# First batch of a spectral mixture-of-experts kernel: fixed load order, stage hand-over through DRAM, deeper input buffers

## The chip, the cores and the metric

The kernel runs on one core of a Trainium2 chip. The metric is the device time of one execution in microseconds (us), the median of several runs. The engines are called as in the profile: PE (matrix products) with its weight loads PEld, DVE (vector), ACT (scalar), POOL (GpSimd) and SP, which computes nothing here and issues most of the DMA transfers.

## What is computed

Eight batches of 3072 tokens by 256 channels go through a spectral filter, then a gated dense block, then a block of eight experts of which each token uses the one with the largest gate value.

```
X = np.fft.rfft(x, axis=1)                       # x: (8, 3072, 256)
y = np.fft.irfft(X * F[None], n=3072, axis=1)    # F: (1537, 256) complex
t = y.reshape(24576, 256)
t = (t @ w_a) * (t @ w_b) @ w_out                # hidden size 1536
e = argmax(t @ w_gate, axis=1)                   # 8 experts
out[n] = gate(n) * eom(n) * (relu(t[n] @ w1[e[n]]) @ w2[e[n]])
```

The weights of the dense block arrive as 64-bit floats; the kernel turns them into 32-bit values, and then into a high and a low half, by integer and float operations on chip.

## The kernel before, in words

The transform of length 3072 is split as 96 by 32. **Stage 1** transforms over the 96 (one product with the 96x96 matrix `f1f`), **stage 2** over the 32, with the filter and the inverse over the 32 (matrices `cr`, three per tile of 128 rows), and a third step (`s3`) inverts over the 96 when a tile of 384 tokens is about to be used.

Batch 0 is alone at the start: nothing else can run before its result is there. `conv_first` (L294) does it. Stage 1 has 16 units: `load_x` brings 192 KB of input (six buffers, tag `xin`), PE multiplies (L338), and ACT copies the result into `stay` (L339), a tile of 96 partitions that lies where weight chunks 4 to 11 come later (tag `wab`). Stage 2 has 12 units (L344 on): `load_a2` regroups rows by two DMAs of 128 KB from `stay` to a 128-partition tile (L329), each of them from four partitions of `stay` to all 128 of the target; `load_c` brings the filter rows `fg` (256 KB) and the matrices `cr` (384 KB); PE makes `psx` (L351); DVE shuffles the filter (L364) and multiplies twice (L367, L368); PE makes `psb` (L376) one unit later; ACT copies it and writes 256 KB to `b_dr` in DRAM (L379, L380). After the last unit `s3_load(0)` reads 384 KB of `b_dr` back (L392), eight products and a split follow (L399, L415), and the first tile of the dense block can start (first product with the name `pa`).

Between the steps of `conv_first` the program advances `weight_steps` (L648). It handles the dense weights in 12 chunks; a chunk is three loads of 256 KB (L663, L667, four buffers `wraw`) and four steps called first, second, third and fourth (L672 to L722), which use ACT, DVE and POOL and, for two transposes and two small products, PE. The program goes through 18 of these steps beside `conv_first`, the rest beside tile 0 of the dense block, in which slot f (12 of them per tile) needs chunk f.

What sets the order: the program is handed to a scheduler which, before anything runs, places the instructions of each engine by its own estimate of when they can start; the order in which they were written is a priority only. On the chip each engine then takes its instructions strictly in the order so found, and waits at the first that isn't ready. That holds for SP too: a DMA that waits for a buffer holds up all DMAs behind it on SP. `manual_schedule` (in the file at L957 for the end of the kernel) keeps an engine in the written order.

After tile 0 the dense block runs 64 tiles, with the convolutions of the other batches between its products, then the experts. None of these lines is changed.

Of the kernel before, what the change touches and what calls it, by code (L numbers as in the profile page):

```python
# [22 lines left out]
# sequence index n = 32 * n1 + n2, frequency k = k1 + 96 * k2  # L23
# [8 lines left out]
# routed tokens: expert e owns rows [e * CAP, (e + 1) * CAP) of the bucket buffer  # L32
# [3 lines left out]
def _phases():  # L36
    """Token counts per weight load, largest first, and how many such groups are sure to exist;
    the last kind has as many as could be needed."""
    out, used = [], 0
    for t, seen in ((2048, SNAP * MT), (1024, SNAP * MT), (512, NTOK)):  # L40
        n = -(-(seen - used - NE * (t - 1)) // t)
        out.append((t, n))
        used += t * n
    t = 256
    out.append((t, (NTOK - used + NE * (t - 1)) // t))
    return out
# [7 lines left out]
# high words, read as float32, of the float64 numbers 2**-126 and just under 2**128  # L54
F64_MIN, F64_MAX = (float(v) for v in np.array([897 << 20, (1151 << 20) - 1], np.int32).view(np.float32))
# batches that go through the convolution together, and the tiles in which they do
ROUNDS = (((1,), 1, 6), ((2, 3), 6, 16), ((4, 5), 16, 32), ((6, 7), 32, 48))
# chunks of the first block's weights that are ready before its first tile
N_EARLY = 3
# chunks whose place is not lent to the first convolution  # L60
F_STAY = FC - N2 * D // 1024
# groups of the last kind at its end that are run only if some token needs them
# [4 lines left out]
def spectral_moe_kernel(ctx: ExitStack, tc: tile.TileContext, a: dict, out: bass.AP):  # L67
# [30 lines left out]
    # by chunk of the hidden size: high and low halves of w_a and w_b  # L98
# [10 lines left out]
    def split3(ps, terms, start, stop):  # L109
        """Products of operands given as (high, low) pairs, all but low * low."""  # L110
        n = len(terms)
        for i, ((lh, ll), (rh, rl)) in enumerate(terms):
            nc.tensor.matmul(ps, lhsT=lh, rhs=rh, start=start and i == 0, stop=False)  # L113
            nc.tensor.matmul(ps, lhsT=lh, rhs=rl, start=False, stop=False)  # L114
            nc.tensor.matmul(ps, lhsT=ll, rhs=rh, start=False, stop=stop and i == n - 1)  # L115
# [5 lines left out]
    a_dr, b_dr = {}, {}  # L121

    def conv_steps(bs):
        """Emission steps of some batches' convolution, up to its inverse over n2; each step
        says whether it is of the tensor engine or of the others."""
        vp = pool["v"]
        nb = len(bs)
        # a unit of stage 2 is one group of rows of two batches, or two groups of one
# [77 lines left out]
        # stage 1  # L206
# [25 lines left out]
        # stage 2 and its inverse  # L232
# [61 lines left out]
    def conv_first():  # L294
        """The convolution of batch 0, before there is other work: the tensor engine has time
        for float32 products, which need no split operands, and for a product more instead of
        an exchange of rows. What stage 1 makes stays on chip, where weights come later."""
# [7 lines left out]
        stay = cp.tile([128, N2 * D], F32, tag="wab", name="stay")[:N1]  # L305

        def load_x(u):
            if u < half:
                xin[u] = vp.tile([N1, 2, D], F32, tag="xin", name="xin", bufs=6)
                nc.sync.dma_start(xin[u], xv[:, 2 * u : 2 * u + 2, :])  # L310

        def load_c(u):
            if u < n_u:
                fg[u] = mp.tile([128, 2, D], F32, tag=("xth", "xtl")[u % 2], name="fg")
                nc.sync.dma_start(fg[u], a["fri"][2 * u : 2 * u + 2].rearrange("t p d -> p t d"))
                if u == 0:
                    # its first row pairs two real frequencies: the real parts come row by row
                    fr0 = vp.tile([128, 2, D], F32, tag="fr", name="fr0")
                    nc.sync.dma_start(fr0, a["frfi"][0:2, :, 0].rearrange("t p d -> p t d"))
                    fg[0] = fg[0], fr0  # L320
                cr[u] = vp.tile([128, 3, 2, 128], F32, tag="cr", name="cr", bufs=6)
                nc.sync.dma_start(cr[u], a["c_first"][u])

        def load_a2(u):
            if u < n_u:
                a2[u] = vp.tile([128, 2, D], F32, tag="xin", name="a2", bufs=6)
                for j in range(2):
                    k = 4 * (2 * u + j)
                    nc.sync.dma_start(a2[u][:, j, :], stay[k : k + 4].rearrange("k (n d) -> k n d", d=D))  # L329

        for u in range(5):
            load_x(u)
        for u in range(half):
            load_x(u + 5)
            if u in (4, 6, 8):
                load_c(u // 2 - 2)
            p = ps_cv("ps1", 2 * D, N1)
            nc.tensor.matmul(p, lhsT=f1f, rhs=xin.pop(u).rearrange("p n d -> p (n d)"), start=True, stop=True)  # L338
            nc.scalar.copy(stay[:, 2 * D * u : 2 * D * (u + 1)], p)  # L339
            yield  # L340
        for u in range(4):
            load_a2(u)
        xx = {}
        for m in range(n_u + 1):  # L344
            load_c(m + 3)
            load_a2(m + 4)
# [87 lines left out]
    def gate_1(i):  # L434
        z = ztile[i]
        lg, og = z[:, :, D : D + NE], z[:, :, D + NE : D + 2 * NE]
        m = small("gm", [128, 3, 1])
        nc.vector.tensor_reduce(out=m, in_=lg, axis=AX.X, op=ALU.max)
        d = small("gd", [128, 3, NE])
        nc.vector.tensor_tensor(out=d, in0=lg, in1=bc(m), op=ALU.subtract)  # L440
        e = small("ge", [128, 3, NE])
        nc.scalar.activation(e, d, AF.Exp)
        # the first of equal maxima: the largest of 8 - index
        r = small("gr", [128, 3, NE])
        nc.vector.scalar_tensor_tensor(
            out=r, in0=d, scalar=0.0, in1=rev.unsqueeze(1).to_broadcast([128, 3, NE]), op0=ALU.is_ge, op1=ALU.mult
        )
        nc.vector.tensor_reduce(out=m, in_=r, axis=AX.X, op=ALU.max)
        oh = small("goh", [128, 3, NE])
        nc.vector.tensor_tensor(out=oh, in0=r, in1=bc(m), op=ALU.is_equal)  # L450
        ob = small("gob", [128, 3, NE], BF16)
        nc.vector.tensor_copy(ob, oh)
        osel = small("gos", [128, 3, NE])
        nc.vector.tensor_tensor(out=osel, in0=oh, in1=og, op=ALU.mult)
        o = small("go", [128, 3, 1])
        nc.vector.tensor_reduce(out=o, in_=osel, axis=AX.X, op=ALU.add)
        eo = small("geo", [128, 3, 1])
        nc.scalar.activation(eo, o, AF.Exp, scale=-1.0)
        gate[i] = (e, oh, ob, eo)
# [19 lines left out]
    def gate_2(i):  # L479
# [18 lines left out]
        # scale = 1 / (sum + 1e-9) / (1 + exp(-o))  # L498
# [63 lines left out]
    def plan(k, start, end):  # L562
        """Expert and first row of each group of kind k among the rows [start, end) of each
        expert; groups past the last one get the dummy rows. Returns the rows left."""
# [57 lines left out]
    def plan_rest(c):  # L622
# [3 lines left out]
        # rows past the last of each expert: no token, scale 0  # L626
# [7 lines left out]
    def load_consts():  # L634
        nc.sync.dma_start(sgn, a["c_sgn"])
        nc.sync.dma_start(f1f, a["c_f1f"])
        nc.sync.dma_start(w3, a["c_w3"])

    def load_consts_2():
        nc.gpsimd.dma_start(f1, a["c_f1"])  # L640
# [7 lines left out]
    def weight_steps():  # L648
        """Float64 weights, one 128-wide chunk of the hidden size at a time: float32 values from
        their bits, exact halves of these, and the gate columns."""  # L650
# [21 lines left out]
        def first(f):  # L672
# [6 lines left out]
            # magnitudes in float32's normal range; the exponent's offset 1023 becomes 127  # L679
# [16 lines left out]
        def third(f):  # L696
# [14 lines left out]
            # gate columns: w_out @ [w_gate | w_output_gate]  # L711
# [24 lines left out]
    # groups that share one load of weights, and their tiles of up to 512 tokens  # L736
# [98 lines left out]
    def l2(n, c):  # L835
# [6 lines left out]
        for j in range(nj):  # L842
            p = psy[n][j // 2][:, 256 * (j % 2) : 256 * (j % 2 + 1)]
            bl = slice(128 * j, 128 * (j + 1))
            # both halves of a bank accumulate; the first product issued there clears it
# [30 lines left out]
    def moe2_slot(n, c, pre=True):  # L876
        """Slot c of tile n of the routed block, with what its successors need."""
# [20 lines left out]

    load_consts()
# [9 lines left out]
    n_first = 8  # L909
    early = 4 * N_EARLY + 7  # L910
    done = 0
    for n, _ in enumerate(conv_first()):
        if n == 4:
            load_consts_2()
# [5 lines left out]
    s3_load(0)  # L920
    for k in range(2):
        s3_mm(0, k)
# [104 lines left out]
    # the last groups, which few distributions of the tokens need  # L1027
# [33 lines left out]
def _constants():  # L1061
# [46 lines left out]
    # of batch 0: also the matrix for the product with the filter's imaginary part, which  # L1108
    # enters the partner's row
# [52 lines left out]
```

## Time and profile before

| | us |
|---|---|
| median of 3 runs (4184.61 to 4190.07) | 4187.19 |
| span of the profiled execution | 4183.0 |
| first product of stage 1 | at 5.57 |
| first product of stage 2 | at 38.09 |
| last product of stage 2 | at 153.47 |
| first product of the dense block | at 167.48 |
| first slot of tile 1 copied | at 221.31 |
| PE busy in the whole span | 4064.7 (97%) |

The profiled execution's span is 4.2 us below the median of the runs; what is worked out on the span is moved by that. The page shows PE as busy nine tenths or more in all slices of 104.6 us but the first two. The chain of work that ended last is not resolved by the page (its shares are zero), so the start of the kernel has to be read from windows, waits and the order of time.

### The profile page before, as it was taken

To read this page: it belongs to the slowest core of one execution; us is meant where nothing else is said; L and a number is where in the kernel's file an instruction comes from. 1 tells how busy PE (TensorE), PEld (TensorE's weight loads), DVE (VectorE), ACT (ScalarE), POOL (GpSimd) and SP (SyncE) were. 2 spreads that over 40 slices of the span, in tenths; PEclk is the share of its full clock that TensorE was granted. 3 is DMA by queue.
4 is the path that set the end of the run, shared out by engine and by line. 5 is a ranking of instruction groups with operands and counts; after the bars stand their busy time and mean duration, and the time that the engine had idled before them with its cause. 6 is when DMAs were issued, how large, how long until landed. Compare 5 with 4: busy or idle time off the path is not lost. (4 is left out here: it accounts for less than half of the span.)

```text
span 4183.0 us, 68755 instructions
## 1 busy us (share of the span) xinstructions
PE 4064.7 (97%) x26500; PEld 3895.0 (93%) x26500; DVE 2059.5 (49%) x4496; ACT 1819.5 (43%) x3832; POOL 724.5 (17%) x672
## 2 busy tenths in 40 slices
PE   5699999999999999999999999999999999999998
PEld 2599999999999999999999999999999999999998
DVE  3556456644465554445554444445433333444575
ACT  2455455544444443444443333333333343444565
POOL 1313013310022210012221000000111111111211
PEclk7699999999999999999999999999999999999999
DMA  5444233312222211222221000001221222234364
GB/s 161 136 129 131 73 99 106 97 55 79 76 69 72 76 58 53 73 69 74 71 66 39 19 22 20 20 20 37 74 69 65 75 95 95 84 128 143 124 218 144
DMA packets 214625, 346.73 MB, mean 83 GB/s; under 512 B 22956, under 2 KB 134285, under 8 KB 214290
## 3 DMA queue, kind: packets, MB, share of 16 engines
q1 hardware_dynamic: 156658, 242.99, 19.2%
q10 hardware_dynamic: 38656, 47.20, 3.6%
q0 software_dynamic: 18976, 52.07, 3.4%
q8 instruction: 210, 3.44, 0.3%
q14 instruction: 125, 1.02, 0.1%
HBM read 237.50 MB, written 102.38 MB: 81 GB/s over the span
## 5 line engine op out<-in xcount | busy, mean ns | idle before, releaser
L540 ACT CAST gh<-g 128x384 fp32r<-128x384 f32 x768 | 394.1, 513 | 833.6 <-DVE g L539 818.8
L539 DVE TENSOR_TENSOR g<-asb,pb 128x384 f32<-128x384 f32 x768 | 424.3, 552 | 632.9 <-PE pb L115 617.1
L115 PE MATMUL po<-wo_h,gl 128*128 128x272 f32 x2304 | 664.6, 288 | 0.0
L114 PE MATMUL po<-wo_l,gh 128*128 128x272 f32 x2304 | 663.4, 288 | 0.0
L118 DVE TENSOR_TENSOR gl<-g,gh 128x384 fp32r<-128x384 f32 x768 | 464.3, 605 | 403.1 <-ACT gh L540 402.3
L113 PE MATMUL po<-wo_h,gh 128*128 128x272 f32 x2304 | 662.5, 288 | 0.0
L532 ACT COPY asb<-pa 128x384 f32<-128x384 f32 x768 | 368.6, 480 | 438.7 <-PE pa L115 437.1
L830 DVE SCALAR_TENSOR_TENSOR hl<-ph,hh 128x512 fp32r<-128x512 f32 (+1 forms) x464 | 284.1, 612 | 528.4 <-ACT hh L829 525.4
L113 PE MATMUL pa<-xth,wab 128*128 128x384 f32 x1536 | 537.2, 350 | 4.0 <-ACT asb L532 3.9
L113 PE MATMUL pb<-xth,wab 128*128 128x384 f32 x1536 | 518.0, 337 | 2.5 <-DVE g L539 2.4
L115 PE MATMUL pa<-xth,wab 128*128 128x384 f32 x1536 | 520.1, 339 | 0.0
L114 PE MATMUL pa<-xtl,wab 128*128 128x384 f32 x1536 | 518.9, 338 | 0.0
L114 PE MATMUL pb<-xtl,wab 128*128 128x384 f32 x1536 | 516.8, 336 | 0.0
L115 PE MATMUL pb<-xth,wab 128*128 128x384 f32 x1536 | 515.6, 336 | 0.0
L829 ACT ACTIVATE hh<-ph 128x512 fp32r<-128x512 f32 (+1 forms) x464 | 250.7, 540 | 547.0 <-PE ph L115 545.9
L503 POOL DMA_INDIRECT zbuf<-z,gpi x192 | 201.1, 1048 | 1636.6 <-ACT asb L532 1054.7
L113 PEld LDWEIGHTS po<-wo_h,gh 128*128 128x128 f32 x2304 | 434.3, 188 | 0.0
L115 PEld LDWEIGHTS po<-wo_h,gl 128*128 128x128 f32 x2304 | 433.3, 188 | 0.2 <-DVE gl L118 0.2
L114 PEld LDWEIGHTS po<-wo_l,gh 128*128 128x128 f32 x2304 | 432.7, 188 | 0.0
L864 POOL DMA_INDIRECT out<-y,z x198 | 204.4, 1032 | 954.2 <-ACT y L863 560.9
L113 PEld LDWEIGHTS pa<-xth,wab 128*128 128x128 f32 x1536 | 289.3, 188 | 16.5 <-ACT asb L532 5.2
L114 PEld LDWEIGHTS pa<-xtl,wab 128*128 128x128 f32 x1536 | 289.7, 189 | 9.5 <-DVE xtl L118 0.3
(178 smaller groups left out, 8078.2 us busy)
## 6 DMA issues: line engine op xcount, KB each, us to landing
raw<-in_moe_w SPq DMA_DIRECT2D x156, 512.0 KB
xin<-in_x SPq DMA_DIRECT2D x128, 192.0 KB
b_dr<-bsb ACTq DMA_DIRECT2D x96, 256.0 KB
bt<-b_dr SPq DMA_DIRECT2D x64, 384.0 KB
z<-zbuf SPq DMA_DIRECT2D x41, 544.0 KB
a_dr<-asb ACTq DMA_DIRECT2D x112, 192.0 KB
a<-a_dr SPq DMA_DIRECT2D x84, 256.0 KB
fg<-in_frfi SPq DMA_DIRECT2D x72, 256.0 KB
```

The source lines that it names most:

```text
L113: nc.tensor.matmul(ps, lhsT=lh, rhs=rh, start=start and i == 0, stop=False)
L114: nc.tensor.matmul(ps, lhsT=lh, rhs=rl, start=False, stop=False)
L115: nc.tensor.matmul(ps, lhsT=ll, rhs=rh, start=False, stop=stop and i == n - 1)
L118: eng.tensor_tensor(out=o, in0=x, in1=h.bitcast(F32), op=ALU.subtract)
L503: nc.gpsimd.indirect_dma_start(out=zbuf, out_offset=bass.IndirectOffsetOnAxis(ap=posi[:, j : j + 1], axis=0), in_=z[:, j, :], in_offset=No ...
L532: nc.scalar.copy(asb, pa)
L539: nc.vector.tensor_tensor(out=g, in0=asb, in1=pb, op=ALU.mult)
L540: nc.scalar.copy(gh, g)
L829: nc.scalar.activation(hh[:, :t], p[:, :t], AF.Relu)
L830: nc.vector.scalar_tensor_tensor(out=hl[:, :t], in0=p[:, :t], scalar=0.0, in1=hh[:, :t].bitcast(F32), op0=ALU.max, op1=ALU.subtract)
L864: nc.gpsimd.indirect_dma_start(out=out, out_offset=bass.IndirectOffsetOnAxis(ap=z[:, j, D + 1 : D + 2].bitcast(I32), axis=0), in_=y, in_of ...
```

## The change

All of it concerns the time before tile 0.

- SP keeps the written order from the first load to `s3_load(0)` (a `manual_schedule` region that is closed after `s3_load(0)`).
- Stage 1 no longer writes to `stay`. ACT copies each product into a small tile (six buffers, tags `gh` and `gl`) and issues a DMA that writes it to a DRAM tensor `a_t` (192 KB each, 16 of them). `load_a2` is now one DMA of 256 KB per unit from `a_t`, 128 rows by two. Weight chunks 4 to 11 no longer share their place with `stay`.
- The input tag `xin` has 8 buffers (`AHEAD`) for 6, in stage 1 and in stage 2; the first eight `load_x` stand at the head, six `load_a2` ahead of stage 2 for four.
- `load_c` for units 0 to 3 stands in stage 1 after the loads of x for units 11, 13, 15 and behind that (it was units 0 to 2, and unit 3 at the head of stage 2); later ones stand behind `load_a2` of their step.
- `f1f` is the first load; `sgn` and `w3` go to the second group of constants, which comes after step 5 for 4.
- `N_EARLY` is 4 for 3 and `n_first` 6 for 8: the program advances 22 weight steps beside `conv_first` for 18, starting two steps sooner; loads of chunks 0 to 7 then stand in SP's fixed order.

```diff
-N_EARLY = 3
+N_EARLY = 4
+AHEAD = 8
@@ conv_first
-        stay = cp.tile([128, N2 * D], F32, tag="wab", name="stay")[:N1]
+        a_t = dp.tile([N1, N2, D], F32, tag="a_dr", name="a_dr")
+        av = a_t.rearrange("k n d -> (k n) d").rearrange("(t p) d -> p t d", p=128)
@@ load_a2
-                a2[u] = vp.tile([128, 2, D], F32, tag="xin", name="a2", bufs=6)
-                for j in range(2):
-                    k = 4 * (2 * u + j)
-                    nc.sync.dma_start(a2[u][:, j, :], stay[k : k + 4].rearrange("k (n d) -> k n d", d=D))
-
-        for u in range(5):
+                a2[u] = vp.tile([128, 2, D], F32, tag="xin", name="a2", bufs=AHEAD)
+                nc.sync.dma_start(a2[u], av[:, 2 * u : 2 * u + 2, :])
+
+        for u in range(AHEAD):
             load_x(u)
         for u in range(half):
-            load_x(u + 5)
-            if u in (4, 6, 8):
-                load_c(u // 2 - 2)
+            load_x(u + AHEAD)
+            if u in (3, 5, 7, 9):
+                load_c((u - 3) // 2)
             p = ps_cv("ps1", 2 * D, N1)
             nc.tensor.matmul(p, lhsT=f1f, rhs=xin.pop(u).rearrange("p n d -> p (n d)"), start=True, stop=True)
-            nc.scalar.copy(stay[:, 2 * D * u : 2 * D * (u + 1)], p)
+            o = mp.tile([128, 2, D], F32, tag=("gh", "gl")[u % 2], name="asb", bufs=3)[:N1]
+            nc.scalar.copy(o.rearrange("p n d -> p (n d)"), p)
+            nc.scalar.dma_start(a_t[:, 2 * u : 2 * u + 2, :], o)
             yield
-        for u in range(4):
+        for u in range(AHEAD - 2):
             load_a2(u)
         xx = {}
         for m in range(n_u + 1):
-            load_c(m + 3)
-            load_a2(m + 4)
+            load_a2(m + AHEAD - 2)
+            if m:
+                load_c(m + 3)
@@ load_consts
-        nc.sync.dma_start(sgn, a["c_sgn"])
         nc.sync.dma_start(f1f, a["c_f1f"])
+
+    def load_consts_2():
+        nc.sync.dma_start(sgn, a["c_sgn"])
         nc.sync.dma_start(w3, a["c_w3"])
-
-    def load_consts_2():
@@ program
+    stack_sp = ExitStack()
+    stack_sp.enter_context(tc.manual_schedule(engines={mybir.EngineType.SP}))
     load_consts()
-    n_first = 8
+    n_first = 6
-        if n == 4:
+        if n == 5:
             load_consts_2()
     nc.sync.dma_start(zbuf[DUMMY : DUMMY + T_B, :].rearrange("(p j) c -> p j c", j=2), fill)
     s3_load(0)
+    stack_sp.close()
```

## Rows read from the trace of the kernel before

**Rows 1.** The page, 40 slices of 104.6 us: busy tenths of PE, granted clock.

```profile
PE   5699999999999999999999999999999999999998
PEclk7699999999999999999999999999999999999999
```

**Rows 2.** Windows by stage: per engine busy us (instructions), granted clock, DMA share, GB/s.

```profile
core 0: us, PE busy (x) PEld busy (x) DVE busy (x) ACT busy (x) POOL busy (x), PEclk, DMA share, GB/s
5.50:30.30 24.80, 19.84 (x32) 6.17 (x32) 2.07 (x6) 8.73 (x15) 0.00 (x0) 0.85 1.00 273
38.00:155.00 117.00, 58.61 (x160) 41.90 (x160) 45.95 (x91) 23.05 (x38) 15.74 (x10) 0.63 0.52 144
155.00:167.50 12.50, 3.75 (x17) 3.51 (x17) 6.70 (x7) 6.29 (x12) 7.35 (x6) 0.50 0.76 212
171.00:206.60 35.60, 32.69 (x206) 31.84 (x205) 29.53 (x52) 23.07 (x49) 14.69 (x9) 0.92 0.17 54
206.60:221.30 14.70, 14.70 (x102) 14.70 (x101) 5.57 (x10) 6.46 (x15) 4.07 (x6) 1.00 0.66 202
221.30:260.00 38.70, 38.70 (x243) 36.63 (x242) 19.75 (x48) 21.73 (x45) 3.32 (x3) 1.00 0.37 113
```

**Rows 3.** Waits, 38 to 155 us: waiter, releaser, total us, times, longest.

```profile
PE psx L351 <- DMA cr<-in_c_first: 48.9, 9, 8.8
...
ACT ws L680 <- DMA wraw<-in_moe_w_out: 21.6, 3, 12.5
...
PE psx L351 <- DMA a<-stay: 14.9, 4, 7.8
```

**Rows 4.** DMA, 33 to 50 us: packets moved; SP's queue with its engine share.

```profile
DMA packets 761, 0.76 MB, mean 45 GB/s; under 512 B 22, under 2 KB 761, under 8 KB 761
...
q1 hardware_dynamic: 761, 0.76, 23.5%
```

**Rows 5.** DMA, 0 to 175 us: SP's queue, ACT's queue: packets, MB, engine share.

```profile
q1 hardware_dynamic: 20450, 25.58, 54.2%
q10 hardware_dynamic: 3264, 3.15, 5.3%
```

**Rows 6.** In order of time, the batch's ends of stage: start us, us, what.

```profile
38.09 1.22 PE L351 MATMUL psx<-a,cr 128*128 128x256 f32 x2 [7.79 <-DMA a<-stay]
...
153.47 1.06 PE L376 MATMUL psb<-qx,cr 128*128 128x256 f32 x2
...
155.18 0.43 ACTq L380 DMA_DIRECT2D b_dr<-bsb  x1
...
159.09 0.34 SPq L392 DMA_DIRECT2D bt<-b_dr  x1
...
167.48 0.69 PE L113 MATMUL pa<-xth,wab 128*128 128x384 f32 x1
```

**Rows 7.** In order of time, batch 1: last write of stage 1, first reads.

```profile
279.31 0.31 ACTq L216 DMA_DIRECT2D a_dr<-asb  x1
...
281.45 6.12 SPq L159 DMA_DIRECT2D a<-a_dr  x5
...
284.33 0.62 ACT L281 CAST a<-a 128x512 fp32r<-128x512 f32 x1 [0.95 <-DMA a<-a_dr]
```

**Rows 8.** In order of time, ACT: copies of slots 0, 3, 7, 11 and the next.

```profile
171.04 0.48 ACT L532 COPY asb<-pa 128x384 f32<-128x384 f32 x1 [2.92 <-PE pa L115]
...
181.03 0.49 ACT L532 COPY asb<-pa 128x384 f32<-128x384 f32 x1
...
200.78 0.48 ACT L532 COPY asb<-pa 128x384 f32<-128x384 f32 x1 [0.96 <-PE pa L115]
...
218.09 0.48 ACT L532 COPY asb<-pa 128x384 f32<-128x384 f32 x1 [1.09 <-PE pa L115]
221.31 0.48 ACT L532 COPY asb<-pa 128x384 f32<-128x384 f32 x1 [1.05 <-PE pa L115]
```

**Rows 9.** Windows of line 694 (POOL, one per chunk): busy, clock, DMA share, GB/s.

```profile
167.50:221.00 53.50, 8.40 (x4) 0.92 0.35 106
```

More of the change, by code (lines that the diff above doesn't have):

```diff
@@ L304, in conv_first @@
         n_u, half = NT // 2, N2 // 2
-        stay = cp.tile([128, N2 * D], F32, tag="wab", name="stay")[:N1]
+        a_t = dp.tile([N1, N2, D], F32, tag="a_dr", name="a_dr")
+        av = a_t.rearrange("k n d -> (k n) d").rearrange("(t p) d -> p t d", p=128)
         def load_x(u):
             if u < half:
-                xin[u] = vp.tile([N1, 2, D], F32, tag="xin", name="xin", bufs=6)
+                xin[u] = vp.tile([N1, 2, D], F32, tag="xin", name="xin", bufs=AHEAD)
                 nc.sync.dma_start(xin[u], xv[:, 2 * u : 2 * u + 2, :])
@@ L634, in load_consts @@
     def load_consts():
+        nc.sync.dma_start(f1f, a["c_f1f"])
+    def load_consts_2():
         nc.sync.dma_start(sgn, a["c_sgn"])
-        nc.sync.dma_start(f1f, a["c_f1f"])
         nc.sync.dma_start(w3, a["c_w3"])
-    def load_consts_2():
         nc.gpsimd.dma_start(f1, a["c_f1"])
```

## Prediction

> **What bounds the kernel now.** The 40 slices come first. PE is busy nine tenths or more in 38 of them, and in these the granted clock is full; only the first two, some 209 us, are loose [rows 1]. The change touches only what lies ahead of the dense block, so the question is how much sooner PE's closed row of work begins, and whether it stays closed. The dense block's first product stands at 167.48 us [rows 6]; every us taken from that is a us of the whole, less what tile 0 gives back.
>
> The windows cut these 167 us into stages [rows 2]. In stage 1 (5.5 to 30.3) the DMA engines are full: share 1.00, 273 GB/s. [...] The waits name DMA for nearly all of PE's idle time, 48.9 us for `cr` and 14.9 for `a` [rows 3]; but a wait is put down to what came last, and all of these are in one queue, so the name doesn't say which is slow. For that I look at a stretch in which only the regrouping of `stay` is in flight, 33 to 50 us: 0.76 MB, 45 GB/s, at an engine share of 23.5% [rows 4]. A share of 23.5% held for 17 us is 4 of 16 engines always busy and 12 idle; each transfer reads four partitions. A unit of 0.262 MB takes 0.262 / 0.045 = 5.8 us in this way, 12 units 70 us. What is queued behind for all 16 engines (0.655 MB of `fg` and `cr` per unit, and weights) can't finish until the four are through. I take this as the bound of stage 2.
>
> **The change part by part.** *Rates.* From 0 to 175 us SP's queue moved 25.58 MB in 54.2% of the 16 engines' time, 94.9 us [rows 5]. The regrouping, 3.15 MB at 45 GB/s on 23.5% of the engines, is 70 x 0.235 = 16.4 us of that. The other 22.4 MB took 78.5 us, so 286 GB/s; ACT's writes took 3.15 MB in 9.3 us, 339 GB/s. The nearest rows to a queue full of 16-engine transfers thus lie at 273 and 339 GB/s.
>
> *Stage 1 and its hand-over.* In SP's fixed order these stand ahead of the first `a2`: x 16 x 0.197 = 3.15 MB, `fg`/`cr` of four units with the extra first row set 2.88, weight chunks 0 to 3 3.15, constants 0.35: 9.5 MB. ACT's 16 writes of `a_t` add 3.15 on the same engines; 12.7 MB in all. Before, about 8.2 MB stood ahead. From 2.5 us, where the first bytes move, 12.7 MB end at 2.5 + 46.5 = 49 us at 273 GB/s and at 40 us at 339. I take 46, nearer to the row of the same stage: stage 2 starts 8 us *later* than the 38.09 of before. The DRAM trip itself does not set this. Batch 1 does the same trip: write issued 279.31, read issued 281.45, data used at 284.33, 5.0 us [rows 7]; behind a stage 1 that ends at 33 or so that is over by 39, under the cover of the loads. If the queue were empty, it would be the bound and stage 2 would start at 39. ACT's 16 issues at 0.31 us [rows 7] are 5 us on an engine that is busy 8.7 of 24.8 us in stage 1 [rows 2]: nothing. The two more input buffers, `f1f` first and the constants two steps later change only the order within a full queue: nothing.
>
> [...] Were the writes free, stage 2 would start at 37 us rather than 46, and the time would be 9 us lower.
>
> *Stage 2.* From then on the queue holds `a2` 3.15, `fg`/`cr` of eight units 5.24, chunks 4 to 7 3.15 and the writes of `b_dr` 3.15, 14.7 MB: 43 us at 339 GB/s, 54 at 273. DVE had 46 us of work in the same stretch, five weight chunks among it (POOL's 10 instructions are two per chunk) [rows 2], and must do it here too. [...] All three lie between 43 and 54; I take 55, 4.6 us per unit, and 3 us for the last unit's own chain.
>
> *Waits that the fixed order adds.* SP now stops at `load_x` until a product has freed a buffer, at `load_c` until the filter four units back is shuffled, and at chunks 4 to 7 until the chunk four back has gone through its second step; behind it wait `a2` and `cr` of later units. `a2` is issued six units ahead and `cr` three, so 14 us at the new pace; that covers most of it. ACT's order can still hold a copy behind a weight step that waits for its load, as before (21.6 us in three waits, [rows 3]). Bounds: 0 and 21.6 us. I take 3 of these, since the chunks now come earlier relative to their steps.
>
> *Tail.* From the last product to the first of the dense block it was 167.48 - 153.47 = 14.0 us (the write, 3.9 us to the reload's issue, and so on [rows 6]), and nothing in it is changed; the loads of weights that shared the queue there are partly gone, so 13.4.
>
> Sum: 46 + 55 + 3 + 3 + 13.4 = 120.4 us for the dense block's first product, 47 us sooner.
>
> *What tile 0 gives back.* Before, the scheduler had run ahead in the idle time: only 4 of 12 chunks had POOL's product still to come after 167.5 [rows 9]. Slots 3 to 7 of tile 0 took (200.78 - 181.03) / 4 = 4.94 us each, slots without weight work 221.31 - 218.09 = 3.22 us [rows 8]. So a chunk left over costs about 1.7 us. With the fixed order chunks 8 to 11 are not even loaded before the reload, and of 4 to 7 I expect two or three to be still under way: six or seven left over. Two or three more at 1.7 us, 4 us back.
>
> Net 47 - 4 = 43 us: span 4183.0 - 43 = 4140; the profiled execution lies 4.2 us under the median, so 4144 us.
>
> **The rivals.** *Weights become the bound of tile 0.* Tile 0 needs chunk f in slot f; for it speaks that DVE was busy 29.5 of 35.6 us while four chunks and the ends of others were worked off [rows 2]. If as many as eight are left and each takes the 4.94 us plus POOL's 2.1 us per product [rows 9] in series, 7 us a slot, tile 0 lasts 8 x 7 + 4 x 3.22 + 2 = 71 us for 221.3 - 171.0 = 50.3. That is 21 back for 4: 4161 us, and to 4172 with some of the 21.6 us of waits.
>
> *All goes at the best rate.* 40 + 43 + 3 + 14 = 100 us for the first product, 4 back: 63 us sooner, 4124 us. For it speaks that later mixes are mostly wide transfers; against it stage 1's own 273.
>
> *The narrow transfers were not the bound; the loads of `cr` and `fg` are.* Three quarters of PE's wait are put down to `cr` [rows 3]. If their just-in-time issue behind freed buffers sets the 9.75 us a unit, the pace stays, and stage 2 starts at 46: 46 + 116 + 13.4 = 175.4, 8 us later than before, and 4 back: *slower*, 4199 us. The point from which it loses is (167.5 - 4 - 13.4 - 46) / 12 = 8.7 us a unit. Against it: the row at 45 GB/s [rows 4], by which the regrouping alone takes 5.8 of the 9.75 us and holds the same queue. [...]
>
> *It doesn't do what it says, or gain and loss cancel:* the scheduler places other engines by its own estimate of the loads, and a misplaced weight step stalls PE as the 12.5 us wait did [rows 3], once per chunk. Four or more of these cancel the 43: 4187 us.
>
> **How the numbers follow.** Forecast 4144 (its own range 4132 to 4156, from the ends of the rates): 0.48. Best rate, 4124: 0.18. Weights bound, 4161 to 4172: 0.20. Cancelled: 0.07. `cr` bound and slower: 0.07. The likeliest is 4144. The range takes in the forecast, the weight rival and most of the best rate: 4118 to 4172. A measurement of this kernel can tell about 0.2% (8.4 us) from no change: faster 0.87, same 0.06, slower 0.07.
>
> **What would show it.** In the changed kernel's windows: DMA share near 1 from 3 to 45 us; first `psx` at 40 to 49 us; no long stretch at a share of 0.2 to 0.25; units 4 to 5.5 us apart; first `pa` near 120; tile 0 about 54 us from its first slot's copy to tile 1's. The forecast is wrong if units stay 8.7 us or more apart, if tile 0 lasts over 65 us, or if PE's slots after tile 1 differ from before.

## The result, and the profile after

The changed kernel takes 4119.05 us in the median (4117.67 to 4122.12), the kernel before 4185.9 beside it: a ratio of 0.9846, interval 0.9832 to 0.9860, 67 us or 1.5% faster. The forecast was 4144 with a range of 4118 to 4172. The sign and the bound were right; the gain was half as large again as forecast (67 for 43), so the time lies 1 us inside the lower end of the range and outside the forecast's own 4132 to 4156.

The two profiled executions differ by less, 4183.0 - 4120.3 = 62.7 us, mostly since that of the changed kernel was the longest of its four (4122.12). The account below is made on the spans. In the order of time the answering lines of [rows 6] are these (start, length, what; SPq and ACTq are DMA issues):

```profile
49.66 4.61 PE L355 MATMUL psx<-a,cr 128*128 128x256 f32 x10
...
92.17 0.59 PE L380 MATMUL psb<-qx,cr 128*128 128x256 f32 x2
...
94.46 0.37 ACTq L384 DMA_DIRECT2D b_dr<-bsb  x1
...
97.22 0.37 SPq L667 DMA_DIRECT2D wraw<-in_moe_w_a  x1
...
98.72 0.36 SPq L396 DMA_DIRECT2D bt<-b_dr  x1
...
110.18 0.47 ACT L419 CAST xth<-ps 128x384 fp32r<-128x384 f32 x1
...
110.70 0.69 PE L115 MATMUL pa<-xth,wab 128*128 128x384 f32 x1 [3.01 <-ACT xth L419]
```

And ACT's copies of slot 0 of tile 0 and slot 0 of tile 1, for [rows 8]:

```profile
114.26 0.48 ACT L536 COPY asb<-pa 128x384 f32<-128x384 f32 x1 [2.92 <-PE pa L117]
...
160.82 0.48 ACT L536 COPY asb<-pa 128x384 f32<-128x384 f32 x1 [1.05 <-PE pa L117]
```

| stretch | before, us | after, us | difference |
|---|---|---|---|
| up to the first psx | 38.09 | 49.66 | +11.6 |
| first psx to last psb | 115.4 | 42.5 | -72.9 |
| last psb to first product of the dense block | 14.0 | 18.5 | +4.5 |
| from there to slot 0 of tile 1 | 53.8 | 50.1 | -3.7 |
| the rest of the span | 3961.7 | 3959.5 | -2.2 |

So all of it is stage 2; stage 1 and the tail became longer, tile 0 a little shorter. The windows by stage (per engine busy us and instructions, granted clock, DMA share, GB/s), which answer to [rows 2]:

```profile
core 0: us, PE busy (x) PEld busy (x) DVE busy (x) ACT busy (x) POOL busy (x), PEclk, DMA share, GB/s
3.70:34.00 30.30, 21.19 (x32) 6.29 (x32) 2.07 (x6) 9.02 (x16) 0.00 (x0) 0.78 0.97 298
49.60:92.50 42.90, 36.85 (x160) 29.95 (x159) 39.09 (x87) 18.54 (x32) 10.21 (x7) 0.94 0.92 302
92.50:110.70 18.20, 3.99 (x18) 3.49 (x16) 16.03 (x14) 10.78 (x19) 13.91 (x8) 0.59 0.75 227
```

The first two stages together, from the first bytes to the last psb:

```profile
2.50:92.50 90.00, 59.87 (x198) 37.67 (x198) 48.72 (x101) 36.49 (x59) 16.02 (x11) 0.81 0.95 306
```

Stage 2, which had a DMA share of 0.52 and 144 GB/s before, now has 0.92 and 302; PE works 36.9 of 42.9 us at a mean granted clock of 0.94 for 0.63. PE's wait for `cr`, 48.9 us in [rows 3], is nearly gone (49 to 111 us: waiter, releaser, total us, times, longest):

```profile
ACT ws L684 <- DMA wraw<-in_moe_w_out: 3.7, 1, 3.7
...
PE psx L355 <- DMA cr<-in_c_first: 1.6, 2, 1.0
```

It had been put down to `cr`, and `cr` is loaded as before, byte for byte. What made it late stood ahead of it in the queue.

### The profile page after: what moved, and what is told of

The parts are those of the page before. It is cut to its first block, busy times and chain, and to the rows that moved or that the text cites. A ratio compares the mean times of both kernels' runs of the same rounds, so it can differ in the third digit from the quotient of the medians.

```text
span 4120.3 us, 68775 instructions
## 1 busy us (share of the span) xinstructions
PE 4043.5 (98%) x26500; PEld 3882.2 (94%) x26500; DVE 2057.9 (50%) x4496; ACT 1819.5 (44%) x3832; POOL 724.7 (18%) x672
```

## The experiments

**Which part carries the gain: one part undone, one part done.** The first kernel keeps order, buffers and early chunks, and goes back to `stay`:

```diff
-        a_t = dp.tile([N1, N2, D], F32, tag="a_dr", name="a_dr")
-        av = a_t.rearrange("k n d -> (k n) d").rearrange("(t p) d -> p t d", p=128)
+        stay = cp.tile([128, N2 * D], F32, tag="wab", name="stay")[:N1]
@@ load_a2
-                nc.sync.dma_start(a2[u], av[:, 2 * u : 2 * u + 2, :])
+                for j in range(2):
+                    k = 4 * (2 * u + j)
+                    nc.sync.dma_start(a2[u][:, j, :], stay[k : k + 4].rearrange("k (n d) -> k n d", d=D))
@@ stage 1
-            o = mp.tile([128, 2, D], F32, tag=("gh", "gl")[u % 2], name="asb", bufs=3)[:N1]
-            nc.scalar.copy(o.rearrange("p n d -> p (n d)"), p)
-            nc.scalar.dma_start(a_t[:, 2 * u : 2 * u + 2, :], o)
+            nc.scalar.copy(stay[:, 2 * D * u : 2 * D * (u + 1)], p)
```

> The changed kernel with one part undone: stage 1 writes to `stay` again and `load_a2` takes two transfers of four partitions each; fixed order, eight buffers and four early chunks stay. If the narrow transfers were the bound, stage 2 is back at 8 to 10 us a unit with stretches at a DMA share of 0.2 to 0.25, and the time is 4165 to 4195 us. If SP's order was the bound, most of the gain stays: 4120 to 4135 us.

4167.04 us, ratio 0.9955 (0.9939 to 0.9972). First and last psx, and the DMA share in tenths over 40 slices of 4.25 us:

```profile
42.22 1.20 PE L354 MATMUL psx<-a,cr 128*128 128x256 f32 x2
...
136.20 1.03 PE L354 MATMUL psx<-a,cr 128*128 128x256 f32 x4
```

```profile
DMA  4989779972222323762544524775689973897200
```

94 us from first to last unit, 8.5 us each, and the row of twos is back as soon as the regrouping starts. Order, buffers and early chunks alone are worth 19 us of the 67. The second kernel is that of before with the way through DRAM alone (the same lines the other way round; free order, six buffers and three early chunks stay):

> The kernel before with one part done: stage 1 goes through DRAM and `load_a2` is one wide transfer; free order, six buffers, three early chunks. If the narrow transfers were the bound, 4120 to 4145 us, units 3.5 to 5.5 us apart. If SP's order was the bound, 4170 us or more.

4123.04 us, ratio 0.9849 (0.9833 to 0.9866).

```profile
44.76 3.62 PE L352 MATMUL psx<-a,cr 128*128 128x256 f32 x8
...
85.69 1.12 PE L352 MATMUL psx<-a,cr 128*128 128x256 f32 x4
...
107.85 0.69 PE L113 MATMUL pa<-xth,wab 128*128 128x384 f32 x1 [2.30 <-ACT xth L416]
```

One part brings 63 of the 67 us. The parts don't add (19 + 63 = 82): with the narrow transfers gone the order has little left to help. The rest of the change, one part undone at a time, for which only the times are needed. Without the fixed order on SP:

```diff
-    stack_sp = ExitStack()
-    stack_sp.enter_context(tc.manual_schedule(engines={mybir.EngineType.SP}))
@@ after s3_load(0)
-    stack_sp.close()
```

> The changed kernel without the fixed order on SP. If the narrow transfers were the bound, it is within 15 us of the changed kernel (4115 to 4135 us) and a little slower, as weights come between. If the fixed order carries the gain, 4150 us or more.

4122.32 us (0.9851, 0.9835 to 0.9868). With six buffers for eight:

```diff
-AHEAD = 8
+AHEAD = 6
```

> The changed kernel with six input buffers for eight (and the loads placed by that number). If the queue is full anyway, within 4 us of the changed kernel: 4115 to 4125 us. If the buffers keep the queue full, stage 1 or 2 is 5 to 10 us longer: 4124 to 4130 us.

4124.27 us (0.9854, 0.9838 to 0.9869). With three early chunks from step 8:

```diff
-N_EARLY = 4
+N_EARLY = 3
-    n_first = 6
+    n_first = 8
```

> The changed kernel with three early chunks from step 8, as before the change. If one chunk more or less at the start is paid in tile 0, within 4 us of the changed kernel: 4115 to 4125 us. If the fourth early chunk is what kept tile 0 short, 4125 to 4130 us.

4122.04 us (0.9852, 0.9838 to 0.9865). All three lie 3 to 5 us above the changed kernel by the medians, 2 to 3 by the ratios, inside the width of their intervals; none of them can be told from no effect.

**Is it the number of engines, or the place that is read?** The changed kernel, with `a_t` padded and read in two transfers of four rows of 32 each:

```diff
-        a_t = dp.tile([N1, N2, D], F32, tag="a_dr", name="a_dr")
-        av = a_t.rearrange("k n d -> (k n) d").rearrange("(t p) d -> p t d", p=128)
+        a_t = dp.tile([N1, N2 + 1, D], F32, tag="a_dr1", name="a_dr", bufs=1)
@@ load_a2
-                nc.sync.dma_start(a2[u], av[:, 2 * u : 2 * u + 2, :])
+                for j in range(2):
+                    k = 4 * (2 * u + j)
+                    nc.sync.dma_start(a2[u][:, j, :], a_t[k : k + 4, :N2, :])
```

> The changed kernel, but `load_a2` reads the DRAM tensor (rows padded so that they can't be merged) in two transfers whose slowest dimension is four. If the number of engines is what costs, these run on 4 of 16 (share about 0.25 where nothing else is queued), the units are 6 to 9 us apart and the time is 4145 to 4185 us. If reading from four partitions of the on-chip memory was what was slow, the time is within 10 us of the changed kernel.

4142.06 us, ratio 0.9895 (0.9878 to 0.9911): 23 us lost, with units 5.6 us apart, between the two outcomes that were expected. From 45 to 62 us (40 slices: share in tenths, GB/s), where almost nothing else is in flight:

```profile
DMA  2222222222222222222222222222325942222422
GB/s 96 94 94 94 96 92 94 94 96 94 92 94 96 94 92 94 96 94 92 94 96 96 92 94 94 96 92 94 113 96 200 373 169 96 94 92 96 133 96 96
```

About four engines again (SP's queue took 26.2% of the 16 engines' time), at an even 94 GB/s. The 45 GB/s from `stay` in [rows 4] is a mean over a stretch that is not even. The kernel before, the same 33 to 50 us in 40 slices:

```profile
GB/s 24 24 24 24 24 29 22 27 24 24 34 53 27 19 27 22 27 22 22 43 43 60 65 48 48 43 46 55 72 51 53 82 84 65 60 72 87 75 55 75
```

It is 26 GB/s up to 41 us and 61 from there on, at nearly the same share (22.3% and 24.5%). In the kernel with `stay` and fixed order the first four slices with a two in the row above (38.25 to 55.25 us) moved 28, 44, 64 and 81 GB/s. So both count. Being narrow costs 23 of the 67 us. With four on-chip partitions as the source the same number of engines moved less than the 94 GB/s, by a factor that changes, and the kernel with `stay` lies another 25 us higher. In the traces the difference lies in stage 2 (first psx to last psb 97.6 us for 64.5, begun 6.1 us sooner); tail and tile 0 are equal within 0.6 us. That kernel also lacks ACT's writes to DRAM, and its weight chunks share their place with `stay` again, for which ACT waited once, 4.6 us; neither was tried alone. The rival by which reading on-chip memory alone was slow falls, and so does "the number of engines alone". Why four partitions are read more slowly than four DRAM rows, and at a changing rate, was not tried.

**What bounds the start now?** The weights begun ten steps later:

```diff
-    n_first = 6
+    n_first = 16
```

> The changed kernel with the weights begun after step 16 for 6, so that none of their loads stands ahead of the first a2. If stage 2's start is set by the bytes queued ahead of it, first psx comes at 38 to 41 us for 49.7, 3.15 MB at 0.3 MB a us. If the start is set by the writes to DRAM and their way back, it stays within 3 us. The end of stage 2 stays within 4 us of 92.5 if the DMA engines bound both stages together, since the same loads come later; then 4112 to 4124 us.

4124.02 us (0.9851, 0.9836 to 0.9866).

```profile
38.05 1.22 PE L355 MATMUL psx<-a,cr 128*128 128x256 f32 x2 [5.53 <-DMA a<-a_dr]
...
91.64 0.59 PE L380 MATMUL psb<-qx,cr 128*128 128x256 f32 x2
```

Stage 2 starts 11.6 us sooner and ends at the same time. What stands ahead of the first `a2` sets when stage 2 starts, but not when it ends. With 3.15 MB of weights out of the way the start follows the way through DRAM: the last row of products of stage 1 runs from 28.83 to 32.53, the first `a2` is issued at 35.29, and the first psx comes 2.8 us behind that. In the changed kernel PE has, ahead of its first psx at 49.66, products of the weights that wait for POOL:

```profile
48.46 0.69 PE L704 MATMUL pt<-ident,ws 128*128 128x128 f32 x2 [3.30 <-POOL ws L698]
```

The same with fewer bytes: the third matrix of `cr` is not loaded, and the second is used in its place:

```diff
-                nc.sync.dma_start(cr[u], a["c_first"][u])
+                nc.sync.dma_start(cr[u][:, :2], a["c_first"][u][:, :2])
-    nc.tensor.matmul(p[:, j], lhsT=c[:, 1 + i, j], rhs=y[:, j], ...)
+    nc.tensor.matmul(p[:, j], lhsT=c[:, 1, j], rhs=y[:, j], ...)
```

> The changed kernel without the third of the three matrices per tile of `cr`: it is not loaded (128 KB less per unit, 1.57 MB in all), and the second stands in for it, so that all instructions stay and only the result of batch 0 is another. If bytes bound everything up to the end of stage 2, the last psb comes 5 us sooner (87 for 92.2) at 0.3 MB a us. If DVE, which was busy 39.1 of the 42.9 us, sets the pace of stage 2, it stays within 2 us. Time 4113 to 4119 us in the first case, since tile 0 can take part of it back, 4119 to 4123 in the second.

```profile
89.03 0.59 PE L380 MATMUL psb<-qx,cr 128*128 128x256 f32 x2
```

The last psb comes 3.1 us sooner for the 5 expected, slot 0 of tile 1 at 156.60, 4.2 us sooner. The whole took 4137.74 us, which can't be used: with batch 0's values its tokens' experts change, and a group that is otherwise skipped at the end runs (26600 products on PE for 26500). The bytes count, but 3 of 5 us say that something else, DVE or the last loads' own time, is close behind. The kernel with three early chunks errs to the other side: it loads one chunk less (0.79 MB, 2.6 us at 0.3 MB a us) and ends stage 2 4.5 us sooner (last psb at 87.65). So bytes alone do not give the end of stage 2, and how much of it is DVE's work on the weights stays open.

**Tail and tile 0.** ACT's split of the first tile's input in the kernel before, and the first product of that input in the changed kernel:

```profile
166.96 0.47 ACT L415 CAST xth<-ps 128x384 fp32r<-128x384 f32 x1
```

```profile
103.96 3.73 PE L403 MATMUL ps<-w,bt 96*128 96x96 f32 x16 [11.20 <-DMA bt<-b_dr]
```

The product comes 10.2 us after the last psb before the change (163.71) and 11.8 after it. ACT's split follows 3.3 us later before (166.96) and 6.2 us later after (110.18): of the 4.5 us by which the tail grew, 1.6 lie ahead of this product and 3.0 at the split. Here ACT too keeps the written order, to the end of that split:

```diff
-    stack_sp.enter_context(tc.manual_schedule(engines={mybir.EngineType.SP}))
+    stack_sp.enter_context(tc.manual_schedule(engines={mybir.EngineType.SP, mybir.EngineType.Activation}))
-    stack_sp.close()
     for k in range(2):
         s3_mm(0, k)
     for k in range(2):
         s3_evac(0, k)
+    stack_sp.close()
```

> The changed kernel with ACT, like SP, in the written order, up to the split of the first tile's input. In the changed kernel that split stood on ACT 4 us behind its data, after weight steps. If these cost the tail, the first product of the dense block comes 4 to 5 us sooner (the tail from the last psb is 13 to 14 us for 18.2); but fewer chunks are ready, and at 1.7 us for each of two to four more left over tile 0 takes 4 to 7 us longer, in sum 4117 to 4125 us. If left-over chunks run in series at 7 us a slot, 4135 us or more.

4121.07 us (0.9846, 0.9832 to 0.9859).

```profile
106.10 0.48 ACT L419 CAST xth<-ps 128x384 fp32r<-128x384 f32 x1 [0.28 <-PE ps L403]
...
159.96 0.48 ACT L536 COPY asb<-pa 128x384 f32<-128x384 f32 x1 [1.05 <-PE pa L117]
```

The split comes 4 us sooner, the dense block's first product 3.2 us (107.47), tile 1 only 0.9. The 4 us were indeed weight steps placed ahead, and they were not lost: of the 3.2 us 1.3 are left at slot 0 of tile 0 (112.94) and 0.9 at tile 1. How much one chunk is worth in tile 0 is read from its products `pg`, four per chunk, inside tile 0. Kernel before, changed kernel, and three early chunks, in this order:

```profile
L720 PE MATMUL pg<-wg,wt 128*128 128x16 f32 x40 | 6.0, 263 | 2.6 <-DVE wt L713 2.6
```

```profile
L724 PE MATMUL pg<-wg,wt 128*128 128x16 f32 x36 | 5.1, 255 | 1.3 <-DVE wt L717 1.3
```

```profile
L724 PE MATMUL pg<-wg,wt 128*128 128x16 f32 x40 | 5.3, 245 | 2.6 <-DVE wt L717 2.6
```

Ten, nine and ten chunks still to be ended; from slot 0 to slot 0 the tile lasts 50.27, 46.56 and 49.27 us. The other kernels in which POOL makes all its products fit: 50.07 with ten (DRAM only, three early chunks), 45.81 to 47.03 with nine (all seven with four early chunks). The count goes with the number of early chunks and not with the length of the tail, which is 15.0 to 19.4 us in those with nine, 14.0 and 18.0 in those with ten. A chunk left over costs 2.7 us where only the early chunks and their start differ (changed kernel and three early chunks). Of these, 1.3 are idle time of PE (1.6 to 2.9 us) and 1.4 more PE time (44.97 to 46.36 us, at a granted clock of 0.98 and 0.97). The kernel before, at 0.95, is 3.7 us longer than the changed one.

**What makes a left-over chunk so dear.** In the changed kernel's tail, DVE's steps on the weights while POOL multiplies, and one of them alone:

```profile
38.53 0.56 DVE L691 TENSOR_SCALAR wraw<-wraw 128x768 int32<-128x768 int32 x1
...
99.97 4.15 POOL L698 TENSOR_TENSOR ws<-wraw,ws 128x768 f32<-128x768 f32 x2
100.22 2.20 DVE L686 TENSOR_SCALAR wraw<-wraw 128x768 f32<-128x768 f32 x1
...
102.45 2.08 DVE L691 TENSOR_SCALAR wraw<-wraw 128x768 int32<-128x768 int32 x1
```

The line at 99.97 is POOL's, two products in a row. A step of 0.56 us lasts about as long as the product beside it. A step that takes 0.96 us alone took 2.61 at the longest (2.63 before the change); the 3.5 us in the expectation below are a row of two such steps (95.40, 3.48 us). Two kernels test this. One leaves the product out (the weights lose their signs):

```diff
-            nc.scalar.activation(high.bitcast(F32), high.bitcast(F32), AF.Abs)
-            nc.gpsimd.tensor_tensor(out=xs[f], in0=high.bitcast(F32), in1=xs[f], op=ALU.mult)
+            nc.scalar.activation(xs[f], high.bitcast(F32), AF.Abs)
```

> The changed kernel without POOL's product of magnitude and sign for the dense block's weights: ACT writes the magnitude to the place of the product, so the signs are left out; loads and all other steps stay. If POOL's two-input products hold up DVE's work on the weights (a DVE step of 0.96 us alone took 2.5 to 3.5 us beside one), the tail and tile 0 get shorter, first slot of tile 1 copied 5 to 12 us before 160.8, and 4107 to 4115 us. If tile 0 is bound by PE alone, within 3 us of the changed kernel.

```profile
148.39 0.48 ACT L536 COPY asb<-pa 128x384 f32<-128x384 f32 x1 [1.05 <-PE pa L117]
```

Tile 1 starts 12.4 us sooner (the whole, 4131.44 us, again has an extra group of experts, so it tells nothing). The other keeps all work and moves POOL's two operations to DVE:

```diff
-            nc.gpsimd.tensor_tensor(out=xs[f], in0=high.bitcast(F32), in1=xs[f], op=ALU.mult)
+            nc.vector.tensor_tensor(out=xs[f], in0=high.bitcast(F32), in1=xs[f], op=ALU.mult)
-            sub(nc.gpsimd, dl, xw, dh)
+            sub(nc.vector, dl, xw, dh)
```

> The changed kernel with POOL's two operations per weight chunk (1.85 and 1.28 us) on DVE. If DVE stands still beside POOL's anyway, it now spends less in sum, and the tail and tile 0 are up to 6 us shorter: 4112 to 4119 us. If the two engines do overlap, DVE has 2 us more per chunk, and it is 4120 to 4130 us.

4116.92 us (0.9839, 0.9826 to 0.9853).

```profile
95.15 0.96 DVE L698 TENSOR_TENSOR ws<-wraw,ws 128x768 f32<-128x768 f32 x1
...
101.91 0.55 DVE L691 TENSOR_SCALAR wraw<-wraw 128x768 int32<-128x768 int32 x1
...
153.56 0.48 ACT L536 COPY asb<-pa 128x384 f32<-128x384 f32 x1 [0.74 <-PE pa L117]
```

DVE makes the product in 0.96 us where POOL took 1.85 and held DVE up, and its step in the tail is back at 0.55 us (line at 101.91); the tail (last psb 93.05, first product 106.05) is 13 us for 18.5, tile 1 starts 7.3 us sooner. The whole is 2 us faster by the medians, with intervals that overlap: not resolved. Last, this with three early chunks:

> The two last findings together: weight work on DVE alone, and three early chunks from step 8. With three early chunks stage 2 ended 4.5 us sooner and tile 0 lasted 2.7 us longer while POOL's work stood in DVE's way. If DVE alone has room for one chunk more in tile 0, slot 0 of tile 1 is copied 2 to 5 us before the 153.6 of the kernel with four chunks on DVE, and 4110 to 4116 us. If a left-over chunk still costs tile 0 about 3 us, no difference to that kernel: 4114 to 4119 us.

4114.83 us (0.9829, 0.9815 to 0.9842).

```profile
150.63 0.48 ACT L536 COPY asb<-pa 128x384 f32<-128x384 f32 x1 [0.72 <-PE pa L117]
```

Tile 1 starts 10.2 us before that of the changed kernel. In the time of the whole it is 4 us faster by the medians and 7 by the ratios, with intervals that overlap (0.9815 to 0.9842 and 0.9832 to 0.9860), so it is the fastest measured, and likely but not shown to be faster than the changed kernel. With POOL out of the way PE has no idle time in tile 0, at a granted clock of 1.00, and one more chunk left over costs 0.8 us there (43.32 us with nine, 42.54 with eight) for the 2.7 above.

## Why the prediction was right, and where it was off

- **The bound: right.** In stage 2 of the kernel before, 117 us or 9.75 a unit, nothing was full by its mean (PE 58.61 us, DMA share 0.52 [rows 2]): four busy DMA engines (by the 23.5% of [rows 4] and the 26.2% above) and a queue behind them. The way through DRAM undone alone gives back 48 us (4167), done alone it brings 63. The 45 GB/s, read as one rate, is a mean of 26 and 61. The rival that the loads of `cr` and `fg` set the pace, and with it the slower outcome, falls.
- **Start of stage 2: 46 forecast, 49.7 measured.** The mechanism holds (later than before, by the bytes ahead): with 3.15 MB of weights out of the way it is 38.05. ACT's writes had to be counted: they took 19.0% of the 16 engines' time from 2.5 to 49.7 us, beside 77.7% for SP's queue. The last 2.3 us are not bytes: the first `a2`, issued at 40.72, landed 6.6 us later, at 47.3, but in PE's order weight products stood first, and they waited for POOL (the line at 48.46 above).
- **Stage 2: 55 + 3 + 3 forecast, 42.5 measured. This is the term that was mis-sized.** I put a start (bytes ahead) and a pace (a unit's bytes, DVE, an estimate of mine for PE, and some margin) in a row, as though the queue began anew at the first `psx`. No run shows the pace I put for PE in the 55: in the 42.9 us it was busy 36.85 at a granted clock of 0.94 (58.61 at 0.63 before [rows 2]), DVE 39.09, at a DMA share of 0.92. The late start costs nothing at the end, as the run with late weights shows. Units were 3.4 us apart for the 4 to 5.5 named as a sign. The sum of the prediction's own bytes would have done better: 12.7 + 14.7 = 27.4 MB at the two rates I had end at 83 to 103 us, while my sum put the end at 107, and the measured 92.2 lies between. At the 306 GB/s of the window from 2.5 to 92.5 us 27.4 MB take 89.5 us; since the rate is read from the very stretch, that confirms the bytes and the full queue (a share of 0.95), not a rate that could have been foretold. The 3 us for misplaced weight steps came in part ahead of stage 2 (above); within it ACT waited 3.7 us for a weight load.
- **Tail: 13.4 forecast, 18.5 measured.** "Nothing in it is changed" was wrong: more weight work fell into it (DVE was busy 16.0 of 18.2 us, before 6.7 of 12.5 [rows 2]), and ACT took weight steps ahead of the split (the run with ACT fixed: 4 us).
- **Tile 0: 4 us back forecast, 3.7 us gained: the sign was wrong.** I held that chunks 8 to 11 can't be loaded before the reload. The region holds only its own instructions in order; the loads of chunks 8 and 9 (87.32 and 97.22) went out ahead of `bt` (98.72). I expected six or seven chunks with POOL's product still to come, for four before; there were three, and nine for ten to be ended, which goes with the fourth early chunk that I had costed at nothing. And a chunk left over costs 2.7 us for my 1.7, which I had read from a mean over slots that had only parts of chunks. The two errors pull opposite ways.
- **The number: in part luck.** At the dense block's first product the errors are +3.7, -18.5 and +5.1 us (110.7 for 120.4), then -7.7 for tile 0, -2.2 for the rest, and -5.4 for the median, which I put 4.2 us above the span and which lay 1.3 below it. Start and tail hid half of the error of stage 2. Two slips change nothing: the last of the forty slices stands at 8 and not at 9 [rows 1], and the 37 us for writes that are free go by 273 GB/s while the 46 beside them go by 292, so their distance is rather 11 us than 9.
- **The rival of weights as the bound:** its 21 us did not come, but its mechanism is there, DVE's work stretched beside POOL's products. It shapes tail and tile 0 together. The best-rate rival came nearest in number (4124); its 43 us for stage 2 are the measured 42.5, its start at 40 and its tail of 14 are not.
- The fixed order, the buffers and the fourth early chunk, costed at next to nothing, are each worth 3 to 5 us by the medians at most, and none of that is resolved. The fourth chunk moves time: without it stage 2 ends 4.5 us sooner and tile 0 lasts 2.7 us longer.
- Open: 2.2 us of the span's difference lie after tile 1's start, where no line is changed; single runs of the changed kernel differ by 4.5 us, and they were not traced further. Open too: the rate of reads from four on-chip partitions, and DVE's share in the end of stage 2.

## What to carry to other kernels

Read the DMA share together with GB/s in a stretch where one kind of transfer is alone: here 23.5% of 16 engines at 45 GB/s [rows 4], an estimate of four engines (0.235 x 16 = 3.8), and `cr`, queued behind, took the blame in the waits (48.9 us, and 1.6 with the wide transfers). Look at the rate slice by slice, too: that mean hid 26 and 61 GB/s. Once transfers are wide and the queue is full (a share of 0.95 here), time a stage by all bytes from the first to the last needed one before trusting start plus pace: 83 to 103 us and 107 here, for 92.2 measured. And an idle gap in front of a full engine may be full of useful work on others, as the tail was (DVE busy 16.0 of 18.2 us). Shortening it moves that work, so tail and next stage have to be costed as one: with ACT fixed 3.2 us won in the tail left 0.9 at tile 1.

## What the runs showed of the hardware

- Transfers from four DRAM rows or four on-chip partitions, in packets of 1 KB and with little else in flight, took 26.2% and 23.5% of the 16 engines' time, an estimate of four busy engines: at an even 94 GB/s from DRAM (23.5 per engine by that estimate), and at 26 to 61 GB/s, 45 in the mean of 17 us, from on-chip partitions (11 per engine).
- DVE's steps of 0.56 us on on-chip weights lasted 2.1 to 2.2 us beside POOL's two-input products of 1.85 us and more; DVE made that product itself in 0.96 us, and with POOL's work moved to it the same steps took 0.55 us.
- Engines waited in their placed order. In the kernel before, ACT's copy of a `psb` whose products ended at 70.66 us began at 79.59, behind a weight step that had waited 12.49 us for its load; SP's load of `fg` at 100.84 waited 2.9 us for DVE, and `cr` behind it went out at 104.38.
